# Casting and transposing x at another place of the batch loop, and three stores in two halves, in an attention and gated feed-forward kernel

## The chip, the cores and the metric

The kernel runs on one core of a Trainium2 chip. The metric is the device time of one execution in microseconds (us). The core has a matrix engine (TensorE: PE in the profile, PEld its weight load), a vector engine (VectorE: DVE), a scalar engine (ScalarE: ACT), GpSimd (POOL) and a queue engine (SyncE: SP) that issues transfers. Each engine works through its own instructions in order and waits on semaphores that the others set.

## The reference

```python
def _attn_ref(x, state):                       # x: 8 x 8 x 512 x 64, state: 8 x 8 x 32 x 64
    scale = 1.0 / np.sqrt(D)
    scores = scale * np.matmul(x, state.transpose(0, 1, 3, 2))
    a = softmax(scores)                        # over the 32 rows of the state
    xread = np.matmul(a, state)
    scores2 = scale * np.matmul(state, x.transpose(0, 1, 3, 2))
    a2 = softmax(scores2)                      # over the 512 rows of x
    sread = np.matmul(a2, x)
    return np.concatenate([xread, sread], axis=2)

def _moe_ref(x, w_gate, w_val, w_out):         # 4352 tokens of 512, inner width 1536
    gate = 1.0 / (1.0 + np.exp(-(x @ w_gate)))
    val = x @ w_val
    return gate * val @ w_out
```

For each of 8 batches and 8 heads, 512 rows of x read from a state of 32 rows, and the state reads from x. The results of the heads are laid side by side, which gives 544 tokens of width 512 for each batch; all of them go through a gated feed-forward layer with a sigmoid gate.

## The kernel before, in words

The kernel writes out the order of every engine's instructions by hand (`manual_schedule`): each engine takes its instructions in the order in which the code names them, and only semaphores hold it back.

Batches are numbered 0 to 7. For a batch, the state is multiplied into the gate and value weights first (`sw_wide`, matmul L272, copied out to `SW`, L310), so that the read of x and the feed-forward layer become one matmul of the attention weights against `SW` (`gv_mm`, L324). The gate is a tanh on ACT (`gv_th`, L334) and one DVE instruction makes the gated value (`gv_glu`, L339). `out_mm` (L355) multiplies by `w_out`; its last part copies the result out on ACT (L359) and issues its store on SP (L361), one store of 128 x 512 numbers for each quarter `c` of a batch. The result tile `res` has four buffers.

The attention of a batch needs x with its columns on the partitions. That is made in three steps:

- `load_x` (L75) reads x of a batch, 1 MB, by SP; the tile `xf` has three buffers.
- `cast_x` (L99) turns it to bf16 in two instructions on POOL; the tile `xb` has two buffers.
- `at_xT_dma` (L123) issues four transposing transfers from `xb` to `xT` on SP.

`S_mm` (L136) multiplies `xT` by the state, and `S_exp` (L141) takes the exponential on ACT. From it come three things: the row sums and the normalised weights `ab` on DVE (`n_sum` L154, `n_mul` L208), the sums over the rows of x (`n_add` L173 and L174 on DVE, `p_fold` L182 to L193 on POOL), and the bf16 copy `Eb` on POOL (`at_Eb`, L147). `aT_dma` (L229) transposes `ab` to `aT` in four transposing transfers on SP. `sr_mm` (L241 to L249) reads the state's share from `Eb` and `xb` on TensorE; `sr_inv` and `sr_fin` (L254, L262) finish it on DVE.

The main loop (L683 on) runs b from 2 to 8, and f from 0 to 11 in each. In step f the gated value of batch b for 128 of the 1536 inner columns is computed, and a third of a quarter of the output of batch b - 1. Beside these, in the loop of b, the batch nb = b + 1 goes through its attention, at steps that are written out:

```python
                if f in (1, 2):
                    S_mm(nb, f - 1, AT)
                    S_exp(nb, f - 1)
                ...
                if f == 3:
                    n_add(nb)
                    at_Eb(nb)
                    p_fold(nb)
                    if nb + 2 < B:
                        load_x(nb + 2, nc.sync)
                if f == 6:
                    aT_dma(nb)
                    if nb + 1 < B:
                        cast_x(nb + 1, pool, 0, 4)
```

So SP has, in the loop of a batch: the four stores of batch b - 1 (at f = 2, 5, 8, 11), the load of x for nb + 2, the four transposes of the attention weights of nb, and the four transposes of x for nb + 1. The loop of b = 8 does the 256 state rows of all batches; after it `out_last` (L375 to L382) computes and stores the last quarter of batch 7 in three pieces.

The completion of a transfer is marked on one of eight semaphores, which the transfers of SP and ACT take in turn; at the end of the program SP waits for all of them, and then all engines meet.

Of the kernel before, what the change touches and what calls it, by code (L numbers as in the profile page):

```python
# [16 lines left out]
def kernel(  # L17
# [14 lines left out]
    nc = tc.nc  # L32
    B, H, S, D = x.shape
# [34 lines left out]
    vec, act, pool = nc.vector.tensor_copy, nc.scalar.copy, nc.gpsimd.tensor_copy  # L68


    def load_x(b, eng, parts=1):
        xf = xfs[b] = stg.tile((128, H, 4, D), FP, name="xf")
        v, n = x[b].rearrange("h (p c) d -> p h c d", c=4), H // parts
        for i in range(parts):
            eng.dma_start(xf[:, n * i:n * i + n], v[:, n * i:n * i + n])  # L75
# [20 lines left out]
    def cast_x(b, cp, lo, n):  # L96
        if b not in xbs:
            xbs[b] = xp.tile((128, 4, H, D), BF, name="xb")
        cp(xbs[b].rearrange("p c h d -> p h c d")[:, lo:lo + n], (xhs if b in xhs else xfs)[b][:, lo:lo + n])  # L99


    def xT_tile(b):
        if b not in xTs:
            xTs[b] = ap_.tile((128, 4, 4, 128), BF, name="xT")
        return xTs[b]
# [14 lines left out]
    def at_xT_dma(b):  # L120
        xT = xT_tile(b)
        for c in range(4):
            nc.sync.dma_start_transpose(xT[:, :, c], xbs[b][:, c].rearrange("p h d -> p (h d)"))  # L123

    def S_mm(b, i, place, jjs=(0, 1)):
        if jjs[0] == 0:
            held["S", b, i] = place[0].tile((128, 4, 2, 2, Ns), FP, name="Sp", tag=place[1])
        ps = held["S", b, i]
        for jj in jjs:
            j = 2 * i + jj  # L130
            for c in range(4):
                if b < 2:
                    e, c2 = c // 2, c % 2 * 2
                    nc.tensor.matmul(ps[:, c2:c2 + 2, e, jj], xTs[b][:, j, c], sTd[:, b, 2 * j + e], start=True, stop=True)  # L134
                else:
                    nc.tensor.matmul(ps[:, c, :, jj], xTs[b][:, j, c], sTz[:, b, j], start=True, stop=True)  # L136

    def S_exp(b, i):
        if b not in E1s:
            E1s[b] = ap_.tile((128, 4, 2, 4, Ns), FP, name="E1")  # L140
        nc.scalar.activation(E1s[b][:, :, :, 2 * i:2 * i + 2].rearrange("p c e j n -> p (c e) j n"),  # L141
                             held["S", b, i].rearrange("p c e j n -> p (c e) j n"), AF.Exp, scale=scale)
# [109 lines left out]
    def sr_inv(b):  # L252
        r2 = held["r2", b] = ap_.tile((128, 4, Ns), FP, name="r2")
        nc.vector.reciprocal(r2, sr_parts(b)[1])  # L254

    def sr_fin(b):
        if ("r2", b) not in held:
            sr_inv(b)
        sr, r2 = sr_parts(b)[0], held["r2", b]
        for e in range(2):  # L260
            rows = slice(e * 64, (e + 1) * 64)
            nc.vector.tensor_tensor(XS[rows, :, b * Ns:(b + 1) * Ns], sr[rows, :, e], r2[rows], ALU.mult)  # L262
# [28 lines left out]
    def sw_wide(b, v):  # L291

        if b not in SWs:
            SWs[b] = fp.tile((128, 2, 2, dff), BF, name="SW", bufs=2)
        lo = 768 * v
        for k, places in enumerate(((OU, AT), (SWP, SWP), (SWP, SWP))):
            pss = [p[0].tile((128, 512), FP, name="swp", tag=p[1]) for p in places]
            if k < 2:
                sw_mm(pss, b, k, lo, 512, 0)
            else:  # L300
                for w in range(2):
                    sw_mm(pss, b, w, lo + 512, 256, 256 * w)
            for e in range(2):
                if k < 2:
                    sw_left[b, v, k, e] = (SWs[b][:, e, k, lo:lo + 512], pss[e])
                else:
                    sw_left[b, v, k, e] = (SWs[b][:, e, :, lo + 512:lo + 768], pss[e].rearrange("p (w n) -> p w n", w=2))

    def sw_cp(b, lo, w, e, cp):
        cp(*sw_left.pop((b, lo, w, e)))  # L310
# [5 lines left out]
    def gv_mm(b, f, place):  # L316
        n = n_of(b)
        fs = slice(f * 128, (f + 1) * 128)
        pss = []
        for w in range(2):  # L320
            ps = place[0].tile((128, 512), FP, name="gvp", tag=place[1])[:, :n]
            if b < B:
                for g in range(2):
                    nc.tensor.matmul(ps, SWs[b][:, g, w, fs], aTs[b][:, :, g], start=(g == 0), stop=(g == 1))  # L324
            else:
                for j in range(4):
                    nc.tensor.matmul(ps, (wg, wv)[w][:, j, fs], XS[:, j], start=(j == 0), stop=(j == 3))  # L327
            pss.append(ps)
        held["gv", b, f] = pss

    def gv_th(b, f):

        th = held["th", b, f] = fp.tile((128, 512), FP, name="th")[:, :n_of(b)]
        nc.scalar.activation(th, held["gv", b, f][0], AF.Tanh, scale=0.5)  # L334

    def gv_glu(b, f):
        if b not in glus:
            glus[b] = fp.tile((128, NF, n_of(b)), BF, name="glu", bufs=2, padded_shape=(128, NF, 512))
        nc.vector.scalar_tensor_tensor(glus[b][:, f], held["th", b, f], 1.0, held["gv", b, f][1], ALU.add, ALU.mult)  # L339
# [3 lines left out]
    def rows_of(b, c):  # L343
        return out[b * SC:b * SC + S].rearrange("(p c) n -> c p n", c=4)[c]

    def out_mm(b, k, place=None):
        c, f0 = k // 3, (k % 3) * 4
        if b == 0:

            c, f0 = k // 6 * 2 + k % 2, k % 6 // 2 * 4  # L350
        if f0 == 0:
            place = place or (SWP if b == B else OU)
            ops[b, c] = place[0].tile((128, 512), FP, name="outp", tag=place[1])
        for f in range(f0, f0 + 4):
            nc.tensor.matmul(ops[b, c], glus[b][:, f, c * 128:(c + 1) * 128], wo[:, f],  # L355
                             start=(f == 0), stop=(f == NF - 1))
        if f0 == 8:
            res = fp.tile((128, 512), FP, name="res", bufs=4)
            nc.scalar.activation(res, ops[b, c], AF.Copy, scale=0.5)  # L359
            if b < B:  # L360
                nc.sync.dma_start(rows_of(b, c), res)  # L361
            else:
                for i in range(4):
                    r0 = (4 * c + i) * SC + S
                    eng = nc.gpsimd if c == 1 and i > 1 else nc.sync
                    eng.dma_start(out[r0:r0 + Ns], res[i * Ns:(i + 1) * Ns])  # L366
# [255 lines left out]
    S_exp(2, 1)  # L622
    S_exp(2, 0)
    out_mm(0, 6, GV)
    gv_glu(0, 6)
    n_sums(2)
# [56 lines left out]
    for b in range(2, B + 1):  # L683
        nb = b + 1 if b + 1 < B else None
        for f in range(NF):

            v, q = divmod(f, 6)
            ahead = nb is not None and q == 0
            if ahead:
                sw_wide(nb, v)  # L690
                sw_cp(nb, v, 0, 0, act)
                sw_cp(nb, v, 0, 1, act)
            for first in (ahead, not ahead):
                if first:
                    gv_mm(b, f, SWP if b == B and f % 2 else GV)
                    gv_th(b, f)
                    gv_glu(b, f)
                elif b < B or f < 9:
                    out_mm(b - 1, f)
            if nb is not None:  # L700
                if f in (0, 8):
                    sw_cp(nb, v, 1, 0, vec)
                if q in (1, 3, 4):
                    k = max(q + 1, 3)
                    sw_cp(nb, v, k // 2, k % 2, act)
# [3 lines that stand above are left out]
                elif f == 9:  # L709
                    sr_mm(nb, AT)  # L710
                    sr_inv(nb)
                elif f == 10:
                    sr_fin(nb)
                if f in (2, 4):
                    n_sum(nb, f // 2 - 1)
                elif f in (5, 6):
                    n_mul(nb, f - 5, nc.vector)
                if f == 3:
                    n_add(nb)
                    at_Eb(nb)  # L720
                    p_fold(nb)
                    if nb + 2 < B:
                        load_x(nb + 2, nc.sync)
                if f == 6:
                    aT_dma(nb)
                    if nb + 1 < B:
                        cast_x(nb + 1, pool, 0, 4)
                        cast_x(nb + 1, pool, 4, 4)
                        at_xT_dma(nb + 1)
    for k in range(6):  # L730
        out_mm(B, k)
    out_last(B - 1, 3)
# [30 lines left out]
```

## Time and profile before

| | |
|---|---|
| median of three runs | 226.16 us (225.31 to 226.33) |
| the profiled execution | 226.29 us |
| its span, first to last instruction | 224.5 us |
| mean granted TensorE clock | 0.997 |
| TensorE (PE) busy | 216.0 us, 96% of the span |
| DVE, ACT, POOL busy | 133.4, 129.5, 79.1 us |
| loop of one batch, b = 2 to 6 | some 23.5 us |

The page gives busy time by engine, a strip of the span in 40 slices, the transfer queues, the chain of work that ended last, the costliest groups of instructions, and the issues of transfers. Beside it the trace answers with the instructions of a stretch in order of time, the waits, and the chain piece by piece. All places in time are microseconds from the start of the span.

### The profile page before, as it was taken

Reading aid. Unit: us, or ns where it says so; the run is one execution under the profiler, and the core shown is the slowest. Engines: PE = TensorE matmul, PEld = TensorE weight load, DVE = VectorE, ACT = ScalarE, POOL = GpSimd, SP = SyncE. Lnnn points to the kernel's source line nnn. Section 1 sums busy time; section 2 is a strip of 40 time slices with the busy share of each in tenths; the row PEclk is TensorE's granted clock in tenths of the full one; section 3 lists DMA queues with packets and bytes.
Section 4 is the critical chain, followed back from the end, with each engine's and each line's share of the span. In section 5 each row is a group of like instructions: output and inputs, shape, how many; then the busy total and the mean of one; then the engine's idle time right before and its main releaser. Section 6 shows DMA issues by size and latency. Waiting matters only on the chain.

```text
span 224.5 us, 4809 instructions
## 1 busy us (share of the span) xinstructions
PE 216.0 (96%) x1843; PEld 110.2 (49%) x1843; DVE 133.4 (59%) x229; ACT 129.5 (58%) x243; POOL 79.1 (35%) x166
## 2 busy tenths in 40 slices
PE   8688999999999999999999999999999999999993
PEld 8553344444444544444444454445445444566753
DVE  3799997977576656765485558573857344322301
ACT  2598886359676557656775757466665444432410
POOL 7986388560038202740256006800560000000001
PEclk9999999999999999999999999999999999999998
DMA  6999999935694253525561441146122112111113
GB/s 96 165 205 255 237 167 136 289 65 151 145 332 136 60 157 97 193 47 98 167 211 35 83 159 54 23 83 131 47 68 75 48 55 79 57 47 47 50 45 97
DMA packets 38439, 26.33 MB, mean 117 GB/s; under 512 B 21040, under 2 KB 33712, under 8 KB 38416
## 3 DMA queue, kind: packets, MB, share of 16 engines
q1 hardware_dynamic: 29168, 17.64, 30.8%
q0 software_dynamic: 8960, 8.19, 21.1%
q8 instruction: 14, 0.23, 0.4%
q10 hardware_dynamic: 288, 0.20, 0.3%
q14 instruction: 9, 0.07, 0.1%
HBM read 18.35 MB, written 8.91 MB: 121 GB/s over the span
## 4 chain that ended last, share of the span: by engine, by line
PE 76%; DMA 11%; POOL 6%; SPq 5%; issue 1%; DVE 0%; POOLq 0%
PE outp L355 36%; PE gvp L324 28%; DMA xf<-in_x_dram 6%; DMA xT<-xb 5%; PE gvp L327 5%; PE swp L272 4%; SPq L123 3%; SPq L229 2%; PE Sp L136 1%; PE srp L249 1%; POOL xh L82 1%; PE outp L375 1%; POOL wg L86 1%; POOL wv L86 1%; POOL xb L99 1%
## 5 line engine op out<-in xcount | busy, mean ns | idle before, releaser
L339 DVE SCALAR_TENSOR_TENSOR glu<-th,gvp 128x512 bf16<-128x512 f32 (+1 forms) x108 | 70.1, 656 | 71.1 <-ACT th L334 57.0
L355 PE MATMUL outp<-wo,glu 128*128 128x512 bf16 x396 | 98.1, 379 | 0.0
L324 PE MATMUL gvp<-aT,SW 128*128 128x512 bf16 x384 | 96.8, 379 | 0.1
L334 ACT ACTIVATE th<-gvp 128x512 f32<-128x512 f32 (+1 forms) x108 | 61.6, 576 | 59.1 <-PE gvp L324 46.1
L324 PEld LDWEIGHTS <-SW 128*128 128x128 bf16 x384 | 36.1, 98 | 44.9 <-issue 4.3
L355 PEld LDWEIGHTS <-glu 128*128 128x128 bf16 x396 | 37.5, 98 | 41.0 <-issue 0.4
L310 ACT CAST SW<-swp 128x512 bf16<-128x512 f32 x74 | 40.9, 586 | 4.1 <-PE swp L272 2.8
L147 POOL CAST Eb<-E 128x256 bf16<-128x256 f32 x32 | 11.5, 409 | 66.0 <-ACT E L141 66.0
L359 ACT ACTIVATE res<-outp 128x512 f32<-128x512 f32 x33 | 19.7, 598 | 18.5 <-PE outp L355 18.4
L366 POOL DMA_DIRECT2D out_dram<-res x2 | 1.1, 536 | 52.5 <-ACT res L359 52.5
L310 DVE CAST SW<-swp 128x512 bf16<-128x512 f32 x22 | 14.8, 683 | 2.5 <-PE swp L272 2.5
L141 ACT ACTIVATE E<-Sp 128x512 f32<-128x512 f32 x16 | 9.5, 602 | 2.0 <-PE Sp L134 1.3
L99 POOL CAST xb<-xf 128x1024 bf16<-128x1024 f32 x9 | 9.1, 1039 | 4.3 <-DMA xf<-in_x_dram 4.0
L187 POOL COPY F<-G 32x128 f32<-32x128 f32 x28 | 9.8, 352 | 1.3
L182 POOL COPY F<-E 64x128 f32<-64x128 f32 x14 | 5.3, 375 | 10.6 <-DVE E L174 10.1
L208 DVE TENSOR_TENSOR ab<-E,ri 128x512 bf16<-128x512 f32 x12 | 8.8, 736 | 0.1
L272 PE MATMUL swp<-wg,sTc 64*32 64x512 bf16 (+1 forms) x192 | 8.4, 328 | 0.0
L154 DVE TENSOR_REDUCE rs<-E 128x16 f32<-128x512 f32 x12 | 8.2, 679 | 0.0
L272 PEld LDWEIGHTS <-sTc 64*32 64x32 bf16 x384 | 4.5, 91 | 7.3 <-issue 5.1
L254 DVE RECIPROCAL r<-srp 128x128 f32<-128x128 f32 x8 | 7.6, 950 | 0.2 <-PE srp L249 0.2
L272 PE MATMUL swp<-wv,sTc 64*32 64x512 bf16 (+1 forms) x192 | 7.4, 322 | 0.0
L327 PE MATMUL gvp<-XS,wv 128*128 128x256 bf16 x48 | 7.2, 273 | 0.0
(76 smaller groups left out, 154.4 us busy)
## 6 DMA issues: line engine op xcount, KB each, us to landing
out_dram<-res SPq DMA_DIRECT2D x31, 256.0 KB, 2.6
xf<-in_x_dram SPq DMA_DIRECT2D x4, 1024.0 KB, 6.5
xf<-in_x_dram POOLq DMA_DIRECT2D x2, 1024.0 KB, 12.1
wo<-in_moe_w_out_dram POOLq DMA_DIRECT2D x3, 512.0 KB, 9.8
xh<-in_x_dram POOLq DMA_DIRECT2D x4, 256.0 KB, 5.0
wg<-in_moe_w_gate_dram POOLq DMA_DIRECT2D x2, 512.0 KB, 11.0
wv<-in_moe_w_val_dram POOLq DMA_DIRECT2D x2, 512.0 KB, 11.7
wg<-in_moe_w_gate_dram POOLq DMA_DIRECT2D x2, 256.0 KB, 9.9
```

What stands on the lines that cost most here:

```text
L99: cp(xbs[b].rearrange("p c h d -> p h c d")[:, lo:lo + n], (xhs if b in xhs else xfs)[b][:, lo:lo + n])
L141: nc.scalar.activation(E1s[b][:, :, :, 2 * i:2 * i + 2].rearrange("p c e j n -> p (c e) j n"), held["S", b, i].rearrange("p c e j n -> p ( ...
L147: nc.gpsimd.tensor_copy(Ebs[b][:, c], E1s[b][:, c])
L187: pool(F[32 * q:32 * q + 32, 1], G[32 * r:32 * r + 32, 0])
L272: nc.tensor.matmul(pss[e][j * Ns:(j + 1) * Ns, o:o + n], sTc[rows, b, j] if b > 1 else sTd[rows, b, 2 * j + e, e], (wg, wv)[w][rows, j, lo ...
L310: cp(*sw_left.pop((b, lo, w, e)))
L324: nc.tensor.matmul(ps, SWs[b][:, g, w, fs], aTs[b][:, :, g], start=(g == 0), stop=(g == 1))
L327: nc.tensor.matmul(ps, (wg, wv)[w][:, j, fs], XS[:, j], start=(j == 0), stop=(j == 3))
L334: nc.scalar.activation(th, held["gv", b, f][0], AF.Tanh, scale=0.5)
L339: nc.vector.scalar_tensor_tensor(glus[b][:, f], held["th", b, f], 1.0, held["gv", b, f][1], ALU.add, ALU.mult)
L355: nc.tensor.matmul(ops[b, c], glus[b][:, f, c * 128:(c + 1) * 128], wo[:, f], start=(f == 0), stop=(f == NF - 1))
L359: nc.scalar.activation(res, ops[b, c], AF.Copy, scale=0.5)
```

## The change

In the loops of nb = 4, 5 and 6, the cast of x for the next batch and its four transposes are issued at step f = 2 instead of f = 6, which puts them ahead of that batch's copy `Eb` and its folds on POOL, and on SP ahead of the four transposes of the attention weights and of the store at f = 5. In the loops of nb = 4 and 5 the load of x for the batch after the next is issued at f = 0 instead of f = 3. The loop of nb = 3 stays as it was. Further, the stores of the first three quarters of batch 6, which are issued in the loop of b = 7, go in two halves of 256 columns each.

```diff
@@ -358,7 +358,9 @@
             res = fp.tile((128, 512), FP, name="res", bufs=4)
             nc.scalar.activation(res, ops[b, c], AF.Copy, scale=0.5)
             if b < B:
-                nc.sync.dma_start(rows_of(b, c), res)
+                n = 256 if b == B - 2 and c < 3 else 512
+                for lo in range(0, 512, n):
+                    nc.sync.dma_start(rows_of(b, c)[:, lo:lo + n], res[:, lo:lo + n])
             else:
                 for i in range(4):
                     r0 = (4 * c + i) * SC + S
@@ -719,14 +721,14 @@
                     n_add(nb)
                     at_Eb(nb)
                     p_fold(nb)
-                    if nb + 2 < B:
-                        load_x(nb + 2, nc.sync)
+                if f == (3 if nb == 3 else 0) and nb + 2 < B:
+                    load_x(nb + 2, nc.sync)
                 if f == 6:
                     aT_dma(nb)
-                    if nb + 1 < B:
-                        cast_x(nb + 1, pool, 0, 4)
-                        cast_x(nb + 1, pool, 4, 4)
-                        at_xT_dma(nb + 1)
+                if f == (6 if nb == 3 else 2) and nb + 1 < B:
+                    cast_x(nb + 1, pool, 0, 4)
+                    cast_x(nb + 1, pool, 4, 4)
+                    at_xT_dma(nb + 1)
```

## The prediction

> Batches are numbered 0 to 7 as in the code; in the loop of batch b the attention of nb = b + 1 and the input of nb + 1 are made ready. What a measurement of this kernel can tell from no change is about 0.5%, 1.13 us.
>
> **What bounds the kernel now.** I read the page's busy times and the stretches by ten microseconds first.
>
> ```profile
> PE 216.0 (96%) x1843; PEld 110.2 (49%) x1843; DVE 133.4 (59%) x229; ACT 129.5 (58%) x243; POOL 79.1 (35%) x166
> ```
>
> ```profile
> 90.00:100.00 10.00, 10.00 (x91) 4.67 (x90) 6.63 (x12) 6.38 (x13) 7.04 (x14) 1.00 0.38 121
> 100.00:110.00 10.00, 9.81 (x86) 4.49 (x85) 5.00 (x9) 6.28 (x13) 0.00 (x0) 1.00 0.48 114
> 110.00:120.00 10.00, 10.00 (x82) 4.46 (x79) 7.35 (x14) 6.31 (x13) 6.55 (x17) 1.00 0.52 160
> ```
>
> The columns are length, then PE, PEld, DVE, ACT, POOL busy, granted clock, DMA share, GB/s. TensorE is the bound: from 40 us to 220 us every stretch has 10.00 of 10, except one. So only three things can pay: the start (not touched), that one hole, and the end. The chain of waits names the hole:
>
> ```profile
> 103.96 3.94 DMA xT<-xb
> 107.90 0.05 issue
> 107.95 0.32 PE Sp L136 x5
> ```
>
> S_mm of batch 5 (L136) waits for the fourth transpose of x, issued on SP behind the four of the attention weights (L229), which wait for DVE. SP's queue there, before the change:
>
> ```profile
> 91.38 0.34 SPq L361 DMA_DIRECT2D out_dram<-res  x1
> 94.95 5.03 SPq L229 DMA_TRANSPOSE aT<-ab  x4
> 100.08 6.07 SPq L123 DMA_TRANSPOSE xT<-xb  x4
> 106.25 3.88 SPq L361 DMA_DIRECT2D out_dram<-res  x3
> ```
>
> How long TensorE really loses is not the 0.19 of the stretch, because modelled ends overlap. Compare the same step in TensorE's timeline with and without the hole (batch 5, then batch 6):
>
> ```profile
> 106.65 1.03 PE L324 MATMUL gvp<-aT,SW 128*128 128x512 bf16 x4
> ...
> 107.95 0.32 PE L136 MATMUL Sp<-sTz,xT 128*128 128x64 bf16 x5 [0.18 <-DMA xT<-xb]
> 108.11 1.03 PE L355 MATMUL outp<-wo,glu 128*128 128x512 bf16 x4
> ...
> 130.48 1.03 PE L324 MATMUL gvp<-aT,SW 128*128 128x512 bf16 x4
> 131.34 0.40 PE L136 MATMUL Sp<-sTz,xT 128*128 128x64 bf16 x8
> 131.58 1.03 PE L355 MATMUL outp<-wo,glu 128*128 128x512 bf16 x4
> ```
>
> From gvp's start to outp's it is 108.11 - 106.65 = 1.46 us with the hole and 131.58 - 130.48 = 1.10 us without: 0.36 us. The period of a batch says the same: that gvp starts at 83.18, 106.65, 130.48, 153.95, so 23.47, 23.83, 23.47.
>
> **The change, part by part.** *Transposes of x ahead (nb = 4, 5, 6).* No instruction is added; two casts, four transposes and, for nb = 4 and 5, one load of x change places on POOL and SP. DVE, ACT and TensorE keep their order instruction for instruction. In the changed order of SP (loop of batch 3, times of the trace before) the load of x6 follows the store at 82.46 and goes at 82.9 instead of 86.39; the store at 85.96 stays; xT of batch 5 goes at 86.3 and takes 4 x 1.27 = 5.1 us, to 91.4; the next store, ready at 91.38, goes at 91.4 to 91.9 (0.52 us behind a transpose, as the row at 81.84 has it); aT still goes at 94.95, because it waits for DVE's product: 3.0 us of SP's wait are left as cover. In the loops of batches 4 and 5 the gaps between those two stores are 109.79 to 115.21 and 133.26 to 138.68, as wide. The transposes fit into a time in which SP waited for ACT; two later stores no longer wait behind them.
>
> The load of x6 takes 6.4 us from issue to landing, so xT of batch 5 may have it ahead of it on the DMA engines. At worst nothing moves until 82.9 + 6.4 = 89.3, and four issues then end at 94.5; aT would start some 0.1 to 0.3 us late. aT lands 2.3 us after its last issue, at 101.1, and gvp needs it at 104.05: 3.0 us more cover. S_mm wants xT at 107.5 and has it by 97. So this costs 0, and if the cover were gone, what is over 3.0 us, three times.
>
> On POOL the casts stand ahead of Eb. The first waits only for x5 (landed at 70), for the buffer that batch 3's state read frees on TensorE (75.95 + 0.47 = 76.4) and for POOL itself, free since 74.6. So it runs at about 76.5 to 78.5 (2 x 1.04 us), while POOL has nothing to do until 87.10:
>
> ```profile
> 72.60 2.02 POOL L99 CAST xb<-xf 128x1024 bf16<-128x1024 f32 x2
> 87.10 1.43 POOL L147 CAST Eb<-E 128x256 bf16<-128x256 f32 x4 [12.47 <-ACT E L141]
> ```
>
> One and two periods later the same: about 99.9 and 123.7, with Eb at 110.93 and some 134.4. Cost 0; cover 8 us. A cast moved this far stands beside DVE's reciprocal (76.74) and its products of the state read, not beside its attention sums.
>
> Gain of this part: the stall of 0.36 us. What is late next? The same steps with the same work ran in 23.47 us in the batches to both sides, so nothing within 0.36 us of it. It is 0 at the low end if the wait is not cured but met again, and 0.36 at the other; I take 0.36, since xT gets over 10 us of room where it lacked 0.36.
>
> Why that one transpose was late bears on this. In the other batches xT lands in 2.5 us; here the view of xT says
>
> ```profile
> DMA to landing us min/median/max: 2.4/3.2/4.2
> ```
>
> and the issue of the fourth took 2.19 us instead of 1.26. The trace's DMA records have two instruction packets there, one of 16 KB from 104.57 for 1.14 us and one of 8 KB from 105.77 for 1.15 us; 15 of the transpose's 16 completion marks came by 107.34 and the last at 107.90. An instruction packet that holds up one engine makes such a stall; packets like that remain after the change, and one can meet another transpose. Against this, the Trainium skill (Runtime: NRT & Kernel Launch, Instruction fetch mechanics) holds that crossing a block of instructions costs one queue step, mostly hidden. By that rule no such stall would come back and the top of my range would be 226.2; the row above speaks for the stall, and here the measurement decides.
>
> *Three stores in halves.* out_mm(6, ...) runs in the loop of batch 7: the stores at 179.09, 184.27 and 189.45 (0.33 us each on SP) become two of 1 KB rows. SP waits 4.8 us before each, and the buffer is wanted only four results later, so three more issues of at most 0.52 us are hidden: cost 0; 1.6 us if SP's wait were gone. What they do move is the end. The eight completion semaphores of SP's and ACT's transfers are used in turn, so three transfers more shift the last store by three places. At the end SP waits for all eight in a fixed order. Before, the last store (issued 221.35, landed 222.99) marks the fifth in that order; from its landing on SP still has this to do:
>
> ```profile
> L758 SPq EVENT_SEMAPHORE  x4: 28/28/28, 223.0 to 223.2; - x4
> L758 SPq DRAIN  x1: 7/7/7, 223.2 to 223.2; - x1
> ```
>
> Four waits, at 223.002, 223.063, 223.122, 223.184: the last store's own and three that have long been met, 0.06 us each. In the changed order the last store has the last semaphore, so the three go by before it lands: 3 x 0.06 = 0.18 us. Bounds: 0 if another engine closes the end (POOL's last drain ends at 222.99, which leaves SP last even so), 0.18 at most. I take 0.18.
>
> **Sum.** 0.36 + 0.18 = 0.54 us. The profiled execution took 226.29 us (span 224.5 and 1.8 around it), so 225.75; it stands 0.13 above the median of 226.16, so 225.6 as a median, 0.24% less: not to be told from no change.
>
> **The rivals.**
> *A stall comes back* (0.20): an instruction packet, or the load now ahead, delays another transpose by the same 0.36 us. For it: the packets at 104.57 and 105.77 now fall into the load of x7. Against: aT has 3.0 us of cover and xT over 10. Time 226.16 - 0.18 = 226.0; with two stalls 226.3.
> *The change does not do what it says* (0.08): POOL or SP holds the moved steps until their old time, or the hole is not in every execution. Then 226.0 to 226.2.
> *POOL and DVE collide* (0.05), the rival on the other side. If the cast ran where it stands in the code, at f = 2 and 3 (86 to 90 us), it would meet DVE's n_add, where DVE goes without a pause from 88.36 to 91.66, so that glu and then TensorE wait. What one costs the other: DVE's product L208 at 92.48, beside POOL's copies, took 0.74 us, and 0.69 elsewhere, so 0.06 by that row; if DVE were held for a whole cast, 1.04. At 1.04 in each of three batches: 225.6 + 3.1 = 228.7, slower by 1.1%; from 0.6 us a batch on it decides (0.54 + 1.13 over three). It needs the cast to begin ten microseconds later than its inputs allow. The Trainium skill (SBUF, "two separate sides") has GpSimd and a DVE instruction with two SBUF inputs lock each other out for a whole instruction; by that rule 1.04 is the price, and the row of 0.06 does not bear it out.
> *More is gained than I see* (0.05): stores that leave earlier shorten something that no row shows, to below 225.0.
>
> **How the numbers follow.** My forecast, 225.6, gets 0.62. The low end is the fastest run before less the gain, 225.31 - 0.54 = 224.8; the high end is the median with one more stall of 0.36 and nothing gained, 226.5. Faster by over 0.5% (below 225.03) needs the gain and a draw like the 225.31 one, or the last rival: 0.12. Slower by over 0.5% (above 227.3) needs the collision or something like it: 0.06. The rest, 0.82, is no change.
>
> **What would show it.** Right: 23.47 us for all three periods of gvp; xT of batches 5 to 7 landed over 10 us before S_mm; the casts near 76.5, 99.9 and 123.7; SP's last transfer followed by one wait at the end, not four; a profiled time near 225.75. Wrong: a wait of TensorE for aT or xT, DVE's sums over 0.7 us beside a cast, or aT issued later than 95.3.

## The result, and the profile after

The changed kernel takes 225.32 us in the median (224.63 to 225.76, 22 runs), the kernel before 225.78 us (225.22 to 226.38, 22 runs, the three shown earlier among them). The medians are 0.46 us apart. The ratio of the two kernels is put at 0.9975, with a 95% interval of 0.9965 to 0.9986: 0.56 us less of the 225.78 (0.32 to 0.79), where 0.54 was worked out. A second comparison on another occasion gave 0.9983 (0.9972 to 0.9995), which is 0.38 us. That is under the 0.5% that one measurement can tell from no change, but with some twenty runs on each side it is seen. One of the 11 runs of a kernel further down (the halves alone) was far slower, 284.29 us, and is left out of its ratio.

The profiled execution has a span of 223.16 us, 1.36 less than the 224.52 before. Only some 0.56 of that belongs to the change (shown below), so I read the places that the prediction named, not the spans. First the stretches (same columns as before):

```profile
90.00:100.00 10.00, 10.00 (x90) 4.71 (x89) 6.66 (x11) 5.85 (x11) 5.38 (x12) 1.00 0.34 81
100.00:110.00 10.00, 10.00 (x90) 4.68 (x89) 5.07 (x10) 6.94 (x13) 1.47 (x3) 1.00 0.56 178
110.00:120.00 10.00, 10.00 (x76) 4.46 (x75) 7.17 (x13) 6.39 (x13) 6.24 (x16) 1.00 0.40 96
```

The 9.81 has become 10.00, and POOL, which did nothing in the middle stretch, now does most of one batch's two casts there (99.22 to 101.24). TensorE's timeline at the scores of batch 5:

```profile
105.86 1.03 PE L324 MATMUL gvp<-aT,SW 128*128 128x512 bf16 x4
106.72 0.40 PE L136 MATMUL Sp<-sTz,xT 128*128 128x64 bf16 x8
106.95 1.03 PE L355 MATMUL outp<-wo,glu 128*128 128x512 bf16 x4
```

From gvp to outp it takes 1.09 us instead of 1.46, without a wait, and the three periods of gvp are 23.47 us each. SP's queue and POOL's timeline of the changed kernel show what was moved:

```profile
85.17 0.34 SPq L363 DMA_DIRECT2D out_dram<-res  x1
85.62 5.69 SPq L123 DMA_TRANSPOSE xT<-xb  x4
91.40 0.52 SPq L363 DMA_DIRECT2D out_dram<-res  x1
94.15 5.03 SPq L229 DMA_TRANSPOSE aT<-ab  x4
```

```profile
75.69 2.03 POOL L99 CAST xb<-xf 128x1024 bf16<-128x1024 f32 x2 [1.85 <-PE srp L249]
86.30 1.44 POOL L147 CAST Eb<-E 128x256 bf16<-128x256 f32 x4 [8.58 <-ACT E L141]
```

The transposes of x fill the time in which SP waited for ACT. The last of them landed at 92.54 (the trace's completion marks), 14.2 us before S_mm wants it; in batches 6 and 7 it is 14.6 and 14.4 us. The cast began as soon as TensorE had read the buffer, and POOL still waits 8.6 us for Eb.

Comparing gvp's starts from end to end between the two profiled executions, the lead of the changed kernel grows in four places only: 0.44 us by 20 us, 0.35 at 38 us (the wait for xT of batch 2, at S_mm), 0.36 at the scores of batch 5, and 0.20 behind the last matmul. The first two lie in code that the change does not touch, where executions of one kernel differ: the unchanged kernel profiled once more had already 0.48 of those 0.79.

### The profile page after: what moved, and what is told of

Its sections match the earlier page's. It is cut to its first block, busy times and chain, and to the rows that moved or that the text cites. A ratio compares the mean times of both kernels' runs of the same rounds, so it can differ in the third digit from the quotient of the medians.

```text
span 223.2 us, 4814 instructions
## 1 busy us (share of the span) xinstructions
PE 215.4 (97%) x1843; PEld 109.9 (49%) x1843; DVE 133.2 (60%) x229; ACT 129.5 (58%) x243; POOL 79.1 (35%) x166
## 4 chain that ended last, share of the span: by engine, by line
PE 92%; DVE 6%; ACT 1%; issue 0%; DVEq 0%
PE outp L355 38%; PE gvp L324 36%; PE swp L272 5%; PE gvp L327 5%; PE warm L391 2%; PE srp L249 1%; PE Sp L136 1%; PE outp L377 1%; DVE ab L208 1%; DVE ab L166 1%; DVE glu L339 1%; DVE rs L154 1%; PE aTp L215 1%; DVE rs L160 1%; DVE xT L118 0%; PE stp L413 0%
## 5 line engine op out<-in xcount | busy, mean ns | idle before, releaser
L327 PE MATMUL gvp<-XS,wg 128*128 128x256 bf16 x48 | 7.2, 273 | 0.0
```

## The experiments

**The parts by themselves.** *The transposes alone:*

```diff
-                n = 256 if b == B - 2 and c < 3 else 512
+                n = 512
```

> The changed kernel without the halves: all stores whole. Theory (the two gains are separate): S_mm of batch 5 does not wait, all three periods of gvp (step f = 1, batches 4 to 7) are 23.47 us, and the end is that of the kernel before: the last store's semaphore is the fifth of eight, so SP has four waits of 0.06 us after it has landed instead of one. Time 0.36 us below the kernel before, 0.16%, and 0.18 above the changed kernel. Rival (the halves do something else that matters, or the gain is all theirs): the period of 23.83 us comes back, or the time equals that of the changed kernel with one wait at the end.

Measured: ratio to the kernel before 0.999 (0.9979 to 1.0001), 225.77 against 225.96 us. TensorE has no wait for xT, and the three periods are equal (23.47 us). *The halves alone*, the kernel before with the first hunk of the change:

> The kernel before with the three stores in halves and nothing moved. Theory: the transposes of x keep their late place, so a wait of TensorE for xT can occur as before (0.36 us in the profiled execution, where an instruction packet meets the transposes; less or none in an execution where it does not); at the end one wait of SP after the last store instead of four, 0.18 us less. Time 0.18 us below the kernel before, 0.08%. Rival (the halves gain nothing, as their landing time is nobody's wait and the end is set elsewhere): the time from the last store's landing to the end is that of the kernel before.

Measured: 0.9997 (0.9985 to 1.0009). TensorE waited for xT of batch 5: gvp to outp 107.75 - 106.23 = 1.52 us, 0.42 over the undisturbed 1.10. *One transfer more*, the changed kernel with all four stores of batch 6 in halves:

```diff
-                n = 256 if b == B - 2 and c < 3 else 512
+                n = 256 if b == B - 2 else 512
```

> The changed kernel with the fourth store of batch 6 in halves too, so one transfer more. Theory (it is the place of the last store among the eight semaphores): the last store now marks the first semaphore in SP's order, so all the other seven are waited for behind it: 7 x 0.06 = 0.43 us more at the end than in the changed kernel, 0.24 more than before. Everything ahead of the end as in the changed kernel. Rival (halves help as such, smaller transfers land sooner): the end is as short as in the changed kernel or shorter.

Measured: 0.9999 (0.9986 to 1.0012); the gain is gone. The times of these three agree with the sum, but each interval holds no change as well, so they could not have told such steps apart by themselves; the profiles do. These are SP's waits for the eight semaphores at the program's end, from the landing of the last store on, first the changed kernel, then the transposes alone, the halves alone, and four halves (number, duration in ns, first and last start):

```profile
L760 SPq EVENT_SEMAPHORE  x1: 28/28/28, 221.8 to 221.8; - x1
```

```profile
L760 SPq EVENT_SEMAPHORE  x4: 28/28/28, 222.5 to 222.7; - x4
```

```profile
L760 SPq EVENT_SEMAPHORE  x1: 28/28/28, 222.6 to 222.6; - x1
```

```profile
L760 SPq EVENT_SEMAPHORE  x8: 28/28/28, 222.4 to 222.8; - x8
```

One, four, one and eight waits, as the last store marks the eighth, fifth, eighth and first semaphore in SP's order. From the start of the last matmul to the end of the span it takes, in the same order, 3.54, 3.73, 3.55 and 4.01 us; in the kernel before, 3.74. Three stores in halves help by 0.19 us, four cost 0.27: what counts is the place in the order, not the halving.

**Why the transpose was late.** *The kernel before once more:*

> The kernel before, unchanged, in another execution. Theory: the packet falls into the fourth transpose of x again, issue over 2 us, and the period of gvp between batches 4 and 5 is 23.8 to 23.9 us. Rival (the hole was an accident of one execution): 23.47 us.

The hole is there, 0.44 us (gvp to outp 1.54). But the issue of the fourth transpose took 1.27 us and not over 2: the packet came 0.96 us after its start, and what was late was the landing. The view of xT for this execution (durations of the issues in ns, the wait, the landing times):

```profile
L123 SPq DMA_TRANSPOSE xT<-xb x4: 1211/1268/1272, 99.6 to 103.5; - x4
...
  DMA xT<-xb: 0.7, 2
...
DMA to landing us min/median/max: 2.4/3.2/4.3
```

*Fewer matmuls at the start*, to bring TensorE's instruction packets to other places:

```diff
     nc.vector.memset(sTz, 0.0)
-    warm(20, SWP)
```

> The kernel before, without 20 of the 68 matmuls that only keep TensorE busy at the start (40 instructions fewer, weight loads counted). Nothing on SP, POOL, DVE or ACT moves, and xT keeps its late place. TensorE's instruction packets of 16 KB come 256 instructions apart, some 18 us, so all come later in the work by about 2.9 us: the packet at 104.57 at about 107.4, after the transposes of x (100.1 to 105.2), and the one at 56.48 at about 59.3, after those of batch 3. Theory (the packet delays the transpose that is being issued): no transpose at those two places takes over 1.35 us, xT of batch 5 lands within 2.5 us of its last issue, at 106.5, TensorE does not wait for it, and the period of 23.83 us is 23.47. Time 0.36 us below the kernel before if the start is no slower. Rival (the place in the queue is what is late): the period of 23.83 us and the wait of TensorE stay.

The expectation was missed where it was aimed: the packet still came at 104.43, in the fourth transpose (2.12 us), and TensorE lost 0.19 us there. Other packets did move, the one at 117.48 to 121.54, into the transposes of batch 5's attention weights, and there a stall appeared that the three profiled executions with x late and all warm-up matmuls did not have. SP's queue and TensorE's timeline of this kernel:

```profile
118.48 6.04 SPq L229 DMA_TRANSPOSE aT<-ab  x4
124.63 5.74 SPq L123 DMA_TRANSPOSE xT<-xb  x4
```

```profile
130.18 1.03 PE L324 MATMUL gvp<-aT,SW 128*128 128x512 bf16 x4
131.04 0.25 PE L136 MATMUL Sp<-sTz,xT 128*128 128x64 bf16 x3
131.64 0.32 PE L136 MATMUL Sp<-sTz,xT 128*128 128x64 bf16 x5 [0.34 <-DMA xT<-xb]
131.79 1.03 PE L355 MATMUL outp<-wo,glu 128*128 128x512 bf16 x4
```

Four transposes of aT take 6.04 us instead of 5.03, the third alone 2.24, all behind them on SP come 1.0 us later, and S_mm of batch 6 waits 1.61 - 1.10 = 0.51 us. So both belong to the hole: the late place, which left x little room, and the packets, which used it up. How little shows in batch 7 of the kernel before: there a packet met the fourth transpose too (2.12 us), the last one landed at 154.62, and S_mm began at 154.81, so nothing was lost by 0.19 us. (It is 0.11, 0.33 and 0.15 us in the other three kernels with x late.) Moving x of batch 7 ahead therefore gained nothing here, but took away a near miss. Time: 1.0016 (0.9996 to 1.0035); two stalls of 0.70 us together where the kernel before has one of 0.36 make 1.0015.

At batch 5 one thing more was added. In the four kernels with x late, 15 of the fourth transpose's 16 completion marks came 0.10 to 0.25 us before S_mm wanted it (0.86 us after gvp's start), and only the last mark, 0.48 to 0.59 us later, made the stall. At batch 7 no mark of the fourth is that late. The trace's records differ there in an 8 KB instruction packet that starts at 105.3 to 105.8, close behind the 16 KB one. So by these rows the 16 KB packet makes the near miss, and at batch 5 the 8 KB one makes it a stall; that was not tried by itself. At batch 6 of the last kernel a 16 KB packet alone was enough.

**The rival on the other side.** The changed kernel with the casts beside DVE's sums:

```diff
                     at_Eb(nb)
+                    if nb > 3 and nb + 1 < B:
+                        cast_x(nb + 1, pool, 0, 4)
+                        cast_x(nb + 1, pool, 4, 4)
+                        at_xT_dma(nb + 1)
                     p_fold(nb)
...
-                if f == (6 if nb == 3 else 2) and nb + 1 < B:
+                if f == 6 and nb == 3:
```

> The changed kernel, but for nb = 4 to 6 the casts of x stand behind Eb and ahead of the folds at step f = 3, with their transposes after them, so that they run where DVE does n_add, n_sum and n_mul. This tries the rival of the prediction that ends on the other side. Theory (by the row of 0.74 against 0.69): DVE's instruction with two inputs from SBUF takes 0.05 to 0.1 us more beside a cast, TensorE never waits, the periods stay 23.47 us, and the time equals that of the changed kernel within 0.1 us. Rival (the lock for a whole instruction): an n_add or n_mul is held for up to 1.04 us in each of three batches, TensorE waits for glu, periods of up to 24.5 us, up to 3.1 us slower.

Measured: 228.44 us, 1.0109 (1.0093 to 1.0125): slower than the kernel before by 2.5 us. The theory, a price of 0.05 to 0.1 us, fell; the rival, a lock for a whole instruction, held. POOL's and DVE's timelines and TensorE's in the first of the three batches:

```profile
88.34 2.48 POOL L99 CAST xb<-xf 128x1024 bf16<-128x1024 f32 x2
```

```profile
88.83 1.09 DVE L173 TENSOR_TENSOR E<-E 128x512 f32<-128x512 f32 x1
90.03 1.07 DVE L174 TENSOR_TENSOR E<-E 128x256 f32<-128x256 f32 x1
91.02 0.67 DVE L339 SCALAR_TENSOR_TENSOR glu<-th,gvp 128x512 bf16<-128x512 f32 x1
```

```profile
91.75 0.59 PE L324 MATMUL gvp<-aT,SW 128*128 128x512 bf16 x2 [0.73 <-DVE glu L339]
```

The sums took 0.68 and 0.42 us before. They lose 0.41 and 0.65, together 1.06 (1.11 in the next two batches). One instruction waits for the other in turn: the first sum ends 0.54 us behind the first cast (89.38), the second cast takes 1.50 us instead of 1.04 and ends at 90.82, and the second sum ends 0.28 us behind it; then glu starts 0.92 us later than the 90.10 before, in an execution that was 0.13 ahead, and TensorE waits for it. By the starts of gvp it loses 0.89, 0.96 and 0.96 us in the three batches, 2.8 us. *The same in four casts of two heads:*

```diff
-                        cast_x(nb + 1, pool, 0, 4)
-                        cast_x(nb + 1, pool, 4, 4)
+                        for lo in range(0, 8, 2):
+                            cast_x(nb + 1, pool, lo, 2)
```

> As e4_cast_beside_sums, where DVE's two sums (L173, L174) took 1.09 and 1.07 us instead of 0.68 and 0.42 and TensorE lost 2.7 us, but each cast of x goes in four instructions of two heads (about 0.55 us each) instead of two of four heads (1.04). Theory (the two engines lock each other out for whole instructions): a sum waits for at most one piece, so the sums together take about 0.5 us more instead of 1.06, TensorE waits 0.3 to 0.5 us a batch, and the time is 1.2 to 1.6 us above the changed kernel. Rival (they share a rate): the sums together take 1.06 us more as before, and the time is again 2.7 us above the changed kernel.

Measured: 0.9989 (0.9974 to 1.0004), 0.1 to 0.3 us above the changed kernel by the ratios and not 1.2 to 1.6. The sums take 0.69 and 0.64, so 0.22 more instead of 1.06 (0.27 in the next two batches), where about 0.5 was expected; the casts pay instead, 2.96 us for the four. TensorE loses 0.67 us in all three batches together, 0.40 of it in one wait for ACT's copy of SW (what made that copy late was not followed). So the rival, a shared rate, fell: the same bytes cost DVE about a quarter when each cast is shorter. That fits a lock for whole instructions, but the size was missed by half. Part of it is the draw of the starts: the first sum, at 88.48, met a cast that ended at 88.61. In the same stretch a glu, whose one input gvp is a result of TensorE, ran beside the third and fourth cast (89.84) and took 0.67 us, no more than elsewhere.

**Further on the start.** Two tries on the wait for xT of batch 2, both on the changed kernel. *Its scores later:*

```diff
+    held["S", 2, 0] = p_sw.tile((128, 4, 2, 2, Ns), FP, name="Sp", tag="swp")
+    gv_mm(1, 1, SWP)
     S_mm(2, 0, SWP)
     gv_glu(1, 4)
     S_mm(2, 1, OU)
-    gv_mm(1, 1, SWP)
```

> The changed kernel, and in the part ahead of the main loop the two matmuls gv_mm(1, 1) go ahead of S_mm(2, 0), whose tile is still taken first, so that xT of batch 2 has 0.86 us more. In six profiled executions TensorE waited there 0.35, 0, 0, 0, 0.17 and 0.57 us. Theory: no wait at that place, 0.2 us less than the changed kernel in the mean, which five rounds will hardly show but the timeline will. Rival (the two matmuls then wait for their own buffers, or the exponentials and sums of batch 2 that are 0.86 us later are waited for): no gain, or up to 0.9 us slower.

Slower, 1.0033 (1.0018 to 1.0048). The wait at the scores is gone, and another has come, as the rival said. From the waits of TensorE in this kernel (total, times, longest):

```profile
PE srp L241 <- POOL hl L193: 1.1, 1, 1.1
```

The folds of batch 2 on POOL start from these scores, and the state read waits for them. *Its load earlier* (`load_x(2, ...)` ahead of `at_Eb(0)`):

> The changed kernel, with the load of x of batch 2 issued on POOL ahead of Eb of batch 0 instead of three instructions later. Theory: it lands 1 to 1.5 us earlier than the 25.8 us of the kernel before, its transposes go on SP as much earlier, TensorE never waits at S_mm of batch 2 (0 to 0.57 us so far), and the time is 0.2 us below the changed kernel in the mean, a ratio of 0.9967 to the kernel before. Rival (the transfers of the weights, which share the 16 engines, come later by as much): TensorE waits for wg or wv between 12 and 30 us, and the time is the same or longer.

Not settled as to time: 0.9985 (0.9962 to 1.0007). The load was issued at 11.21 instead of the changed kernel's 12.42, but took 14.5 us to land instead of 12.4, and the casts began at 25.80 instead of 24.97. TensorE waited 0.4 us for xT all the same, and 0.8 us for `wv`, as the rival said. *The changed kernel beside them:*

> The changed kernel, unchanged, beside e6_scores_later on the same chip: 0.54 us below the kernel before by the two gains, a ratio of 0.9976; the periods 23.47 us, one wait of SP at the end. The start may differ by some tenths of a microsecond between executions, whatever the kernel.

0.9983 (0.9972 to 0.9995), no wait for xT at batch 5. No variant is shown to be better than the changed kernel. The earlier load of x (f = 0) was not run by itself.

## Why the prediction was right, point by point

- *The time.* The forecast was 225.6, the median 225.32. Most of the difference is in the start: the sum began from a median of three runs, 226.16, and 22 runs of the same kernel put it at 225.78. That the gain of 0.56 came within 0.02 of the sum is luck, as its interval is 0.24 us to either side; that each of the two terms was found at its place is not.
- *The stall of 0.36 us.* The kernels with x at its late place lost 0.36, 0.44, 0.42 and 0.19 us there in four profiled executions; all eight with x ahead lost none. Reading it off the timeline (1.46 - 1.10) and the period was needed: the wait that the trace puts down is 0.18. One reading behind it was wrong: it was not so that xT lands in 2.5 us in all other batches. In batches 3 and 7 of the kernel before the third transpose took 4.37 and 4.24 us to land, since a packet came there as well.
- *The end.* Predicted 0.18 by three waits of 0.06, measured 0.20 (3.74 to 3.54), and shown by the two other places of the last store. The waits themselves show it; what comes behind them varies. In the kernel with the casts in four, the last store has the eighth place too, but it takes 3.10 us, for the meeting of the engines behind the waits was 0.44 us shorter.
- *No cost on SP.* aT was issued at 94.15, which is the old 94.95 less the 0.79 by which that execution was ahead: unmoved. The transposes of x took 5.69 instead of the 5.1 worked out, because a packet at 87.32 fell into the second; the cover, still 2.2 us from the store behind them to aT, took it.
- *No cost on POOL.* The casts ran from 75.7, 99.2 and 122.7, with the execution ahead by 0.79 to 1.15: the 76.5, 99.9 and 123.7 forecast.
- *A stall comes back:* it did not in any of the eight, though in each of them packets met transposes of x in their new place.
- *POOL and DVE collide:* here one reading was wrong. I took 0.06 us as the price (0.05 by the row: 0.739 less 0.687), by a DVE product that ran beside POOL's copies on 32 rows, and held that this row did not bear out the lock of the Trainium skill (SBUF, "two separate sides"). I had looked at DVE's side alone. It was POOL that waited, in the same stretch of the kernel before:

```profile
L187 POOL COPY F<-G x4: 279/286/657, 92.1 to 93.4; 32x128 f32<-32x128 f32 x4
```

The copy that took 657 ns is the third: it began at 92.71, inside the product of 92.48 to 93.22, and ended 0.15 us behind it; it takes 657 ns in the next three batches too. Made to happen with casts of 1.04 us, the price was 1.06 us of DVE and up to 0.96 of TensorE in each batch, near the 1.04 of the rival; its 3.1 us were 2.8. The rule of the Trainium skill agrees with the trace. The small chance was right for the other reason alone: where the cast runs is decided by its inputs, ten microseconds ahead of its place in the code. There it ran beside DVE's reciprocal, which took 0.951 us against 0.950 before.

- *The instruction packets.* The Trainium skill (Runtime: NRT & Kernel Launch, Instruction fetch mechanics) calls the crossing of a block of instructions mostly hidden. The trace agrees for the engine that fetches, TensorE: in the changed kernel the stretches with the packets at 104.44 and 116.22 are busy 10.00 of 10. It is another matter for a transposing transfer that a packet meets, by the numbers below.

## What to carry to other kernels

An engine that is busy 96% of the time can still lose tenths of a microsecond to a wait. Find them by the cadence of equal steps, and give the transfer that is late room in a wait that its queue has anyway. Before moving an instruction into idle time of POOL, look at what DVE does in that very time: here casts of 1.04 us on POOL cost DVE's sums, with both inputs in SBUF, 0.41 and 0.65 us, and in shorter pieces less. When looking for such a price, compare the rows of both engines, as either may be the one that waits. And at the program's end it matters which semaphore the last transfer marks: from the eighth place to the first it was 0.47 us here.

## What the runs showed of the hardware that was not expected

Over the twelve profiled executions 576 transposing transfers were issued. Each execution has 14 instruction packets of 16 KB. I take them for TensorE's, which has 1,843 matmuls and as many weight loads, where the page counts fewer than 250 instructions for each other engine. In 44 of the transfers such a packet began between 0.3 us before and 0.9 us after the issue's start: 42 of these took 1.54 to 2.74 us, two 1.17 and 1.24. The other 532 have a median of 1.24 us, and eleven of them are over 1.35, the longest 1.61. A packet that comes later still delays the landing (the unchanged kernel's second execution). In the kernel before, 15 of the third transpose's 16 marks came by 105.13 and the last at 106.89; after that, at 107.15, came the first mark of the fourth. One part out of 16 that was behind held up the whole next transpose. The same stands in the three other kernels with x late: the third transpose's last mark came at 106.50 to 106.57, and the first of the fourth 0.23 to 0.38 us later. That the fetch moved in some places and not in others when 40 instructions were taken away was not explained.
